# Chunked retention two blocks sooner, and a reordered start, in a retention plus maxout feed-forward kernel

## The chip, the cores and the metric

The kernel runs on one core of a Trainium2 chip. TensorE multiplies matrices into PSUM, VectorE, ScalarE and GpSimd do elementwise work, and SyncE issues most of the transfers between HBM and SBUF. Each engine works through its own queue in order; semaphores order them against each other. The time is device microseconds of one execution. Before the change it is 754.58 us, the median of 12 runs (753.28 to 757.65).

## The reference

```python
def _attn_ref(q, k, v):                    # each (8, 8, 576, 64): batch, heads, sequence, head size
    scores = scale * np.matmul(q, k.transpose(0, 1, 3, 2))
    gamma = 1.0 - 2.0 ** (-5.0 - np.arange(H, dtype=np.float32))
    rel = pos[:, None] - pos[None, :]
    Dmat = np.where(rel >= 0, gamma[:, None, None] ** rel[None, :, :], 0.0)
    return np.matmul(scores * Dmat[None], v)

x = attn_out.transpose(0, 2, 1, 3).reshape(B * S, H * D)          # (4608, 512)
h = np.maximum(np.maximum(x @ w1, x @ w2), x @ w3)                # w1, w2, w3: (512, 768), float64
out = h @ w_out                                                   # w_out: (768, 512), float64
```

Queries, keys and values are float32. The four weight matrices arrive as float64 and are turned into float32 on the chip, by bit operations.

## The kernel before, in words

**Blocks and tiles.** The 4608 rows are cut into 36 blocks of 128 rows (`C`), four blocks (`CPT`) to a tile of 512 rows (`NT`), nine tiles. A sequence has 576 rows, so a block may begin or end in the middle of one. Blocks go through retention, which leaves `xT`; then `ffn(t)` does a tile's three up products, their maximum and the down product.

**Retention of a block in full form** (blocks 0 to 7, lines 258 to 430). `transposes` turns `k` and `q` with TensorE (block 7 with VectorE), and ScalarE copies the result out of PSUM; `decay` multiplies the values by a power of gamma on GpSimd; `scores` makes 128x128 scores per head, which VectorE masks (`st`); `state` makes the product of keys and values that the next blocks need, `keep` adds it to the carried state on VectorE and scales it on GpSimd; `values` multiplies masked scores by values (line 393) and adds the carried state times queries (line 406). `output` scales that into `xT`.

**Retention in chunked form** (from block `BY_CHUNKS` = 8). A block is two chunks of 64. `chunk_scores` makes 64x64 scores (`sk`, line 307) and chunk states (`kv`, line 310), VectorE masks the one (line 314) and adds the other into `stacked` states (lines 322 to 328), with a GpSimd product for every second chunk; `chunk_values` multiplies (lines 424 and 431). `q` and `k` come from HBM in 32-wide pieces (`load_blocks`), so that VectorE can transpose them in 32x32 squares; `k` is loaded a second time as it lies. Blocks from `BY_PE` = 7 on are transposed by VectorE. `carry(8)` brings the full-form state into the stacked form.

**Weights.** `load_weights(n)` issues the next `n` of 24 blocks of 128 float64 rows or columns, 512 KB each; two make a piece pair (`Two(n)`, n from 0 to 11; the last three belong to `w_out`). `convert_all` is a generator whose steps go to VectorE and ScalarE: exponent (line 630) with ScalarE's low word (632), fraction (639) with ScalarE's two steps (638, 641), whole (644), sign (648), product (656), which leaves float32 weights and issues the loads of two later blocks. `convert(n)` takes n steps. Pairs 0 to 2 are converted in halves, the others in one.

**Tile 0.** It is done plainly: nine units of two up products each (`up_plain`, four 512-column products of 3.5 us in sum, line 784, then a copy by ScalarE for the first weight matrix or a maximum by VectorE for the others), then `downs_plain` (line 771). Unit u takes the weights of pair u. Tiles 1 to 8 use sums of weights, inputs and hidden values that cut the number of products (`up`, `downs`, lines 760 and 557).

**Order.** It is written by hand: a preamble does blocks 0 to 3 and the first conversion steps; then for each tile t, `steps(t + 1)` lists twelve groups of loading and retention steps of the next tile's blocks, and between the groups the generator `ffn(t)` is advanced by one unit. What the program lists first stands first in each engine's queue, and on SyncE's queue transfers stand in that same order.

```python
    load_weights(1)        # preamble; before this: load(0) to load(3), of which load(3) also has one
    load(CPT)
    load_weights(4)
```

Of the kernel before, what the change touches and what calls it, by code (L numbers as in the profile page):

```python
# [45 lines left out]
ALU = mybir.AluOpType  # L46
PSUM = bass.MemoryType.PSUM

C = 128
NT = 4 * C  # L50
NH = NT // 2
BY_PE = 7
BY_CHUNKS = 8
AHEAD = 3
FILL = 160
PARTS = 11
# [25 lines left out]
def kernel(  # L82
# [21 lines left out]
    NDC = DM // P  # L104
    NF = DF // P
    CPT = NT // C
    assert B * S % C == 0 and S % D == 0 and BY_CHUNKS % CPT == 0 and S >= C and N % NT == 0 and NT % P == 0 and 2 * D == P and NP == NDC

    const = ctx.enter_context(tc.tile_pool(name="const", bufs=1))
    raw = ctx.enter_context(tc.tile_pool(name="raw", bufs=AHEAD + 1))  # L110
# [14 lines left out]

    gk = const.tile([C, H], FP32, name="gk")
    gs_of = const.tile([P, H], FP32, name="gs_of")
    gs = const.tile([P, NP], FP32, name="gs")  # L130
# [1 line left out]
    const.tile([P, FILL // 4], FP32, name="fill")  # L132
    gq = const.tile([P, NP, C], FP32, name="gq")
    nc.scalar.dma_start(gk[:], key_decay)
    nc.vector.memset(one[:], 1.0)
    nc.scalar.copy(first[:], one[:])

# [31 lines left out]
    def spans(g):  # L169

        row = 0
        while row < C:
# [1 line left out]
            n = min(C - row, S - pos)  # L174
            yield row, b, pos, n
            row += n

    def half(j):
        return slice(D * j, D * (j + 1))

    def place(g, c):

# [39 lines left out]
                        t[r:r + 32, :, e, :],  # L222
                        src[b, :, pos:pos + 32, 32 * a:32 * a + 32].rearrange("h p i -> p h i"))

    def load(g):
        if g >= BY_PE and ("q", g) not in raws:
            load_blocks(g, *range(C // 32))
        for n, src in (("k", k), ("q", q), ("v", v)) if g < BY_PE else (("k", k), ("v", v)):
            if n == "v" and g == CPT - 1:
                load_weights(1)  # L230
            bufs = {"k": 3, "q": 2, "v": 4}[n]
            pool, bufs = (raw0, 1) if n != "v" and g < BY_PE and g % (bufs + 1) == bufs else (raw, bufs)
            if n == "v":
                t = vpool.tile([C, H, D], FP32, tag="v", name="vraw")
            else:
                t = pool.tile([C, H, D], FP32, tag=n, name=n + "raw", bufs=bufs)
            raws[n, g] = t
            for row, b, pos, m in spans(g):
                nc.sync.dma_start(t[row:row + m], src[b, :, pos:pos + m, :].rearrange("h p d -> p h d"))
# [100 lines left out]
    def state_factors():  # L340
        for j in range(2):
            nc.scalar.copy(gs_of[half(0), j::2], gs[half(j)])
# [386 lines left out]
    def convert(n):  # L729
        for _ in range(n):  # L730
            next(converting, None)
# [44 lines left out]
                    nc.sync.dma_start(out[t * NT + m * P:t * NT + (m + 1) * P, :], osb[:])  # L776
            yield

    def up_plain(t, h, fb, i):
        ps = (ps_x, ps_y)[fb % 2].tile([P, NT], FP32, tag="xy"[fb % 2], name="up")  # L780
        first_of_all = t == 0 and (fb, i) == (0, 0)
        for cols in (slice(0, NT - C), slice(NT - C, NT)) if first_of_all else (slice(0, NT),):
            for dc in range(NDC):
                nc.tensor.matmul(ps[:, cols], lhsT=w_sb[i, fb][:, dc * P:(dc + 1) * P], rhs=xT[t][:, dc, cols],  # L784
                                 start=dc == 0 and cols.start == 0, stop=dc == NDC - 1,
                                 skip_group_check=first_of_all)
        if i > 0:
            return lambda: nc.vector.tensor_tensor(h[:, fb, :], h[:, fb, :], ps[:], op=ALU.max)
        return lambda: nc.scalar.copy(h[:, fb, :], ps[:])

    def ffn(t):

        h = hpool.tile([P, NF, NT], FP32, tag="h", name="h")
        if t == 0:
            for fp, i in units:
                for fb in (2 * fp, 2 * fp + 1):
                    maximum = up_plain(t, h, fb, i)
                    if CPT not in qks:
                        maximum()
                        transposes(CPT)  # L800
                        convert(4)
                        continue
                    if (fp, i) == units[-1]:
                        maximum()
                        convert(2)
                        continue
                    convert(4 if (fp, i) in units[:2] else 2)
                    maximum()
                yield
            convert(3)  # L810
            for fb, _ in enumerate(downs_plain(t, h)):
                convert(2 if fb < 2 else 4 * len(pieces))
                if fb == 2:
                    while_converting.close()
                    late["pool"] = ctx.enter_context(tc.tile_pool(name="late", bufs=1))
                    late_room()
                    sums_of_outs()
                elif fb > 2:
                    chore({3: 4, 4: 0, 5: 2}[fb])
                if fb in (1, 3):  # L820
                    yield
            yield
            return
        if t == 1:
            spread.append(True)
            weight_sums(0)
            weight_sums(2)
        plain = 1 if t == 1 else None
        order = (1, 0, 2) if t == 1 else (0, 2, 1)
        total = sum(48 if fp == plain else 2 * len(PRODUCTS) for fp in order)  # L830
        count = parts = 0
        for fp in order:
            if fp != plain:
                while fp not in summed_fp:
                    chore()
            for step, cost in enumerate(up_plain_all(t, h, fp) if fp == plain else up(t, h, fp)):
                if fp == plain:
                    chore(4 if step == 4 else 8)
                elif step % 4 == 1 or step % 4 == 3 and len(urgent) > (2 if t == 1 else 6):
                    chore(len(urgent) > 0)  # L840
                elif step % 4 == 2 and chores and (t > 1 or NF // 2 - 1 not in summed_fp):
                    chores.popleft()()
                if step % 3 == 2:
                    scale()
                count += cost or 1
                if count * (NF // 2 * 3) >= (parts + 1) * total:
                    parts += 1
                    yield
            sums_of_hidden(h, fp)
            if fp == plain:  # L850
                weight_sums(fp)
        chore(len(urgent))
        for n, _ in enumerate(downs(t, h, order)):
            chore(4)
            scale(2)
            if n in (1, 3):
                yield
        yield

    def up_plain_all(t, h, fp):  # L860
        for fb in (2 * fp, 2 * fp + 1):
            for i in range(3):
                up_plain(t, h, fb, i)()
                yield 8


    warm(6)
    for g in range(CPT):
        load(g)
        if g == 1:  # L870
            for j in range(2):
                nc.sync.dma_start(gs[half(j)].unsqueeze(2), state_decay[half(j), :, D * j:D * j + 1])
    load_weights(1)
    load(CPT)
    load_weights(4)
    decay(0)
    transposes(0)
    for c in range(2):
        for b in range(2):
            nc.scalar.dma_start(gq[half(c), b::2, :], out_decay[half(b), NP // 2 * c:NP // 2 * (c + 1), :])  # L880
    warm(2)
    scores(0)
    transposes(1)
# [4 lines left out]
    scores(1)  # L888
    first_output()
    transposes(2)  # L890
    state_factors()
    decay(2)
    state(1)
    keep(1)
    values([1], [1])
    transposes(3)
    decay(3)
    scores(2)
    scores(3)
    state(2)  # L900
    keep(2)
    convert(2)
    values([2], [2])
    convert(2)
    values([3], [3])
    convert(4)
    keep(3)
    decay(CPT)
    convert(2)

    def steps(t):

# [11 lines left out]
        if t == 1:  # L924
            a, b, c, d = range(CPT, 2 * CPT)
            at(0, (load, b))
            at(1, (scores, a), (state, a), (keep, a))
            at(2, (transposes, b), (decay, b), (load, c), (load_weights, 2))
            at(3, (scores, b), (load_blocks, d, 0))
            at(4, (decay, c), (load_blocks, d, 1, 2))  # L930
            at(5, (values, [a, b], [b, c]), (load_blocks, d, 3), (load, d))
            at(6, (keep, c), (transposes, c), (load_blocks, d + 1, 0))
            at(7, (transposes, d), (decay, d), (load_blocks, d + 1, 1, 2))
            at(8, (scores, c), (scores, d), (load_blocks, d + 1, 3), (load, d + 1))
            at(9, (load_blocks, d + 2, 0, 1))
            at(10, (decay, d + 1), (load_blocks, d + 2, 2))
            at(11, (values, [c, d], [d]), (load_blocks, d + 2, 3), (load, d + 2),
               (transposes, d + 1))
            return todo
        for n in range(0, CPT, 2):  # L940
            a, b, m = CPT * t + n, CPT * t + n + 1, 6 * (n // 2)
            first_pair = a == BY_CHUNKS
            s = m + 2 if first_pair else m + 1
            at(m - (t == 2 and n > 0), (transposes, b))
            if first_pair:
                at(m, (decay, b), (load, a + 2), (carry, a))
            at(s, (scores, a), (scores, b), (load, b + 2))
            at(s + 1, (decay, a + 2))
            at(s + 2, (decay, b + 2))
# [60 lines left out]
```

## Time and profile before

| | |
|---|---|
| median of 12 runs | 754.58 us |
| the profiled execution | 753.82 us |
| its span, first to last instruction | 751.8 us |
| TensorE clock granted | 1.00 |
| HBM read, written | 48.76 MB, 9.44 MB |
| first up product starts | 24.90 us |
| last product of tile 0's down ends | 123.68 us |
| VectorE transposes of block 7 | 0.70 and 0.67 us |
| largest wait of TensorE | 1.5 us |

A line of a timeline has the start, the length, the engine, the line of the program, the operation, output and inputs by their names with the shape, the number of instructions merged, and in brackets the idle time before it with what ended it. TensorE takes two instructions for each float32 product of the program. A line of waits has the engine and operation that waited, what it waited for, and then microseconds in total, how often, and the longest. A line of windows has the stretch, its length, the busy time of TensorE, its weight loads, VectorE, ScalarE and GpSimd with instruction counts, the clock, the busy share of the DMA engines and the GB/s moved.

### The profile page before, as it was taken

Reading aid. Unit: us, or ns where it says so; the run is one execution under the profiler, and the core shown is the slowest. Engines: PE = TensorE matmul, PEld = TensorE weight load, DVE = VectorE, ACT = ScalarE, POOL = GpSimd, SP = SyncE. Lnnn points to the kernel's source line nnn. Section 1 sums busy time; section 2 is a strip of 40 time slices with the busy share of each in tenths; the row PEclk is TensorE's granted clock in tenths of the full one; section 3 lists DMA queues with packets and bytes.
Section 4 is the critical chain, followed back from the end, with each engine's and each line's share of the span. In section 5 each row is a group of like instructions: output and inputs, shape, how many; then the busy total and the mean of one; then the engine's idle time right before and its main releaser. Section 6 shows DMA issues by size and latency. Waiting matters only on the chain.

```text
span 751.8 us, 16566 instructions
## 1 busy us (share of the span) xinstructions
PE 744.8 (99%) x6728; PEld 608.1 (81%) x6728; DVE 509.6 (68%) x856; ACT 319.7 (43%) x645; POOL 83.3 (11%) x103
## 2 busy tenths in 40 slices
PE   9899999999999999999999999999999999999998
PEld 7545545588888888888888888888888888888887
DVE  3998987857866765686567746775667656763662
ACT  3574531155245433644254335542454245414441
POOL 3110122002000100011010101010101010100000
PEclk9999999999999999999999999999999999999999
DMA  9996842515142514242343224232515151000001
GB/s 230 224 245 135 224 91 73 97 17 99 44 93 43 94 39 96 50 76 52 72 86 67 61 66 91 48 67 67 96 27 95 44 98 31 1 30 29 0 1 57
DMA packets 230204, 59.30 MB, mean 79 GB/s; under 512 B 210800, under 2 KB 228848, under 8 KB 230128
## 3 DMA queue, kind: packets, MB, share of 16 engines
q1 hardware_dynamic: 229264, 57.91, 35.7%
q8 instruction: 53, 0.87, 0.5%
q10 hardware_dynamic: 864, 0.33, 0.2%
q14 instruction: 23, 0.19, 0.1%
HBM read 48.76 MB, written 9.44 MB: 77 GB/s over the span
## 4 chain that ended last, share of the span: by engine, by line
PE 97%; DVE 1%; DMA 1%; SPq 0%; issue 0%; ACT 0%; ACTq 0%; DVEq 0%
PE a L760 19%; PE b L760 16%; PE dx L557 11%; PE up L784 11%; PE c L760 8%; PE dz L557 6%; PE e L760 5%; PE d L760 5%; PE sk L307 3%; PE down L771 3%; PE dy L557 3%; PE o L424 2%; PE o L431 2%; PE s L285 1%; PE kv L310 1%; PE o L393 1%
## 5 line engine op out<-in xcount | busy, mean ns | idle before, releaser
L748 DVE TENSOR_TENSOR part<-part 128x512 f32<-128x512 f32 x161 | 111.2, 691 | 107.8 <-ACT part L745 105.4
L745 ACT COPY part<-b 128x512 f32<-128x512 f32 x115 | 67.4, 586 | 154.0 <-PE b L760 154.0
L748 DVE TENSOR_TENSOR h<-h,part 128x512 f32<-128x512 f32 x115 | 79.6, 693 | 28.9 <-ACT h L745 24.9
L784 PE MATMUL up<-xT,w 128*128 128x512 f32 (+2 forms) x200 | 84.9, 579 | 1.5 <-DVE w L656 1.5
L745 ACT COPY part<-a 128x512 f32<-128x512 f32 x92 | 53.9, 586 | 49.4 <-PE a L760 49.1
L784 PEld LDWEIGHTS up<-xT,w 128*128 128x128 f32 x200 | 36.7, 190 | 43.7 <-issue 39.9
L760 PE MATMUL a<-s,w 128*128 128x256 f32 x276 | 70.9, 379 | 0.0
L760 PE MATMUL b<-s,n 128*128 128x256 f32 x276 | 70.8, 379 | 0.0
L189 ACT ACTIVATE vraw<-vraw,gk 128x64 f32<-128x64 f32 x208 | 65.5, 346 | 1.6 <-DMA vraw<-in_v_dram 1.6
L760 PEld LDWEIGHTS b<-s,n 128*128 128x128 f32 x276 | 52.4, 190 | 7.1
L760 PEld LDWEIGHTS a<-s,w 128*128 128x128 f32 x276 | 52.4, 190 | 7.1
L527 POOL TENSOR_TENSOR H<-h 128x256 f32<-128x256 f32 x24 | 20.2, 842 | 310.1 <-DVE h L748 310.1
L760 PE MATMUL c<-xT,w 128*128 128x256 f32 x184 | 49.1, 389 | 0.0
L760 PE MATMUL b<-xT,n 128*128 128x256 f32 x184 | 47.2, 379 | 0.0
L760 PE MATMUL d<-s,w 128*128 128x256 f32 x184 | 47.2, 379 | 0.0
L324 POOL TENSOR_TENSOR s<-s,gs_of 64x512 f32<-64x512 f32 x21 | 22.4, 1069 | 211.1 <-DVE s L322 209.2
L557 PE MATMUL dx<-To,H 128*128 128x256 f32 (+1 forms) x204 | 44.9, 370 | 0.0
L760 PE MATMUL e<-xT,w 128*128 128x256 f32 x184 | 43.5, 379 | 0.0
L760 PE MATMUL a<-xT,n 128*128 128x256 f32 x184 | 43.5, 379 | 0.0
L557 PEld LDWEIGHTS dx<-To,H 128*128 128x128 f32 x204 | 36.6, 190 | 4.9
L760 PEld LDWEIGHTS e<-xT,w 128*128 128x128 f32 x184 | 35.0, 190 | 5.2 <-issue 0.2
L760 PEld LDWEIGHTS b<-xT,n 128*128 128x128 f32 x184 | 35.0, 190 | 4.8
(122 smaller groups left out, 1287.6 us busy)
## 6 DMA issues: line engine op xcount, KB each, us to landing
bits<-in_moe_w_dram SPq DMA_DIRECT2D x36, 256.0 KB, 5.6
out_dram<-osb SPq DMA_DIRECT2D x35, 256.0 KB, 2.1
kraw<-in_k_dram SPq DMA_DIRECT2D x32, 256.0 KB, 3.0
vraw<-in_v_dram SPq DMA_DIRECT2D x32, 256.0 KB, 3.5
qraw<-in_q_dram SPq DMA_DIRECT2D x224, 32.0 KB, 2.2
kxraw<-in_k_dram SPq DMA_DIRECT2D x224, 32.0 KB, 2.1
bits<-in_moe_w_out_dram SPq DMA_DIRECT2D x6, 512.0 KB, 6.0
qraw<-in_q_dram SPq DMA_DIRECT2D x6, 256.0 KB, 4.4
```

Source lines behind the costliest of these rows:

```text
L189: scaling.popleft()()
L307: nc.tensor.matmul(s[half(c), h, :], lhsT=kT[half(c), h, :], rhs=qT[half(c), h, :], start=True, stop=True)
L324: nc.gpsimd.tensor_tensor(new, new, factor, op=ALU.mult)
L424: nc.tensor.matmul(o[m][half(c), n, u, :], lhsT=vds[g][half(m), h, :], rhs=sts[g][half(m), h, :], start=n == 0 and u == 0, stop=place(g, m ...
L431: nc.tensor.matmul(o[m][half(c), n, u, :], lhsT=stacks[g][half(m), h, :], rhs=qks[g]["q"][half(m), h, :], start=False, stop=True, skip_gro ...
L527: urgent.append(lambda: (pool(s3, a11, a21, op=ALU.subtract), pool(s4, a12, s2, op=ALU.subtract)))
L557: nc.tensor.matmul(o, lhsT=hS[n](fp)[:, m * P:(m + 1) * P], rhs=late["T"][n][:, fp, cols], start=first and fp == order[0] and (m == 0 or l ...
L745: nc.scalar.copy(of[step], ps[step[0]][:])
L748: nc.vector.tensor_tensor(of[dst], a, b, op=op)
L760: nc.tensor.matmul(ps[chain][:, e, :], lhsT=factor(w, 2 * fp + e), rhs=xS[t][x], start=n == 1 and e == 0, stop=ends, skip_group_check=True)
L771: nc.tensor.matmul(b[:], lhsT=h[:, fb, m * P:(m + 1) * P], rhs=w_sb["out", fb], start=(fb == 0), stop=(fb == NF - 1))
L784: nc.tensor.matmul(ps[:, cols], lhsT=w_sb[i, fb][:, dc * P:(dc + 1) * P], rhs=xT[t][:, dc, cols], start=dc == 0 and cols.start == 0, stop= ...
```

## The change

Blocks 6 and 7 go over to the chunked form (`BY_CHUNKS` 8 to 6), and block 6 is transposed by VectorE (`BY_PE` 7 to 6). `carry` runs for block 6. The schedule of tile 1's blocks follows: block 6's loads become 32-wide pieces, no full state of blocks 6 and 7 is made, and two more conversion steps are taken in group 5.

The start is reordered: the state factors `gs` and half of the output factors `gq` are issued on ScalarE's queue earlier; the first weight block stands before block 2's values on SyncE, the second before block 3's values, two more before block 4; block 2 is scored before block 3 is transposed; conversion steps are spread between. The first two up products are each cut into 384 and 128 columns (`first_ups`), and the last block of the tile gets its state and values between them, so that the 384-column parts need blocks 0 to 2 alone.

```diff
-BY_PE = 7
-BY_CHUNKS = 8
+BY_PE = 6
+BY_CHUNKS = 6
...
     nc.scalar.dma_start(gk[:], key_decay)
+    for j in range(2):
+        nc.scalar.dma_start(gs[half(j)].unsqueeze(2), state_decay[half(j), :, D * j:D * j + 1])
...
+    def first_ups(h):
+
+        g = CPT - 1
+        rest0, copy0 = up_plain(0, h, 0, 0, g * C)
+        convert(2)
+        state(g)
+        convert(2)
+        values([g])
+        keep(g)
+        convert(2)
+        rest1, copy1 = up_plain(0, h, 1, 0, g * C)
+        convert(2)
+        for step in (rest0, copy0, rest1, copy1):
+            step()
+        decay(CPT)
+        transposes(CPT)
+        convert(4)
...
             for fp, i in units:
+                if (fp, i) == units[0]:
+                    first_ups(h)
+                    yield
+                    continue
                 for fb in (2 * fp, 2 * fp + 1):
-                    maximum = up_plain(t, h, fb, i)
-                    if CPT not in qks:
-                        maximum()
-                        transposes(CPT)
-                        convert(4)
-                        continue
-                    if (fp, i) == units[-1]:
+                    maximum, = up_plain(t, h, fb, i)
+                    if (fp, i) == units[-1] and fb % 2:
                         maximum()
                         convert(2)
-                        continue
-                    convert(4 if (fp, i) in units[:2] else 2)
-                    maximum()
+                    else:
+                        convert(4 if (fp, i) == units[1] else 2)
+                        maximum()
...
     warm(6)
-    for g in range(CPT):
-        load(g)
-        if g == 1:
-            for j in range(2):
-                nc.sync.dma_start(gs[half(j)].unsqueeze(2), state_decay[half(j), :, D * j:D * j + 1])
+    load(0)
+    load(1)
+    load(2, "kq")
     load_weights(1)
+    load(2, "v")
+    load(CPT - 1, "kq")
+    load_weights(1)
+    load(CPT - 1, "v")
+    load_weights(2)
     load(CPT)
-    load_weights(4)
+    load_weights(2)
     decay(0)
-    transposes(0)
-    for c in range(2):
+
+    def output_factors(c):
         for b in range(2):
             nc.scalar.dma_start(gq[half(c), b::2, :], out_decay[half(b), NP // 2 * c:NP // 2 * (c + 1), :])
+
+    output_factors(0)
+    transposes(0)
+    output_factors(1)
...
     values([1], [1])
-    transposes(3)
-    decay(3)
     scores(2)
-    scores(3)
+    decay(CPT - 1)
+    convert(2)
     state(2)
     keep(2)
+    convert(1)
+    values([2], [2])
+    transposes(CPT - 1)
+    convert(1)
+    state_factors()
     convert(2)
-    values([2], [2])
-    convert(2)
-    values([3], [3])
-    convert(4)
-    keep(3)
-    decay(CPT)
-    convert(2)
+    scores(CPT - 1)
...
             at(0, (load, b))
-            at(1, (scores, a), (state, a), (keep, a))
-            at(2, (transposes, b), (decay, b), (load, c), (load_weights, 2))
-            at(3, (scores, b), (load_blocks, d, 0))
-            at(4, (decay, c), (load_blocks, d, 1, 2))
-            at(5, (values, [a, b], [b, c]), (load_blocks, d, 3), (load, d))
-            at(6, (keep, c), (transposes, c), (load_blocks, d + 1, 0))
-            at(7, (transposes, d), (decay, d), (load_blocks, d + 1, 1, 2))
-            at(8, (scores, c), (scores, d), (load_blocks, d + 1, 3), (load, d + 1))
+            at(2, (scores, a), (state, a), (keep, a), (transposes, b), (decay, b), (load_weights, 2))
+            at(3, (scores, b), (load_blocks, c, 0, 1))
+            at(4, (load_blocks, c, 2, 3), (load, c))
+            at(5, (values, [a, b], [b]), (convert, 2), (load_blocks, d, 0, 1))
+            at(6, (carry, c), (transposes, c), (decay, c), (load_blocks, d, 2, 3), (load, d))
+            at(7, (transposes, d), (decay, d), (load_blocks, d + 1, 0, 1))
+            at(8, (scores, c), (scores, d), (load_blocks, d + 1, 2, 3), (load, d + 1))
             at(9, (load_blocks, d + 2, 0, 1))
             at(10, (decay, d + 1), (load_blocks, d + 2, 2))
-            at(11, (values, [c, d], [d]), (load_blocks, d + 2, 3), (load, d + 2),
+            at(11, (values, [c, d]), (load_blocks, d + 2, 3), (load, d + 2),
                (transposes, d + 1))
...
             if first_pair:
-                at(m, (decay, b), (load, a + 2), (carry, a))
+                at(m, (decay, b), (load, a + 2))
```

More of the change, by code (lines that the diff above doesn't have):

```diff
@@ L106 @@
     CPT = NT // C
-    assert B * S % C == 0 and S % D == 0 and BY_CHUNKS % CPT == 0 and S >= C and N % NT == 0 and NT % P == 0 and 2 * D == P and NP == NDC
+    assert B * S % C == 0 and S % D == 0 and BY_CHUNKS % 2 == 0 and S >= C and N % NT == 0 and NT % P == 0 and 2 * D == P and NP == NDC
     const = ctx.enter_context(tc.tile_pool(name="const", bufs=1))
@@ L124, with half @@
     ctx.enter_context(tc.manual_schedule())
+    def half(j):
+        return slice(D * j, D * (j + 1))
     gk = const.tile([C, H], FP32, name="gk")
@@ L176, in spans @@
             row += n
-    def half(j):
-        return slice(D * j, D * (j + 1))
     def place(g, c):
@@ L223, in load_blocks, with load @@
                         src[b, :, pos:pos + 32, 32 * a:32 * a + 32].rearrange("h p i -> p h i"))
-    def load(g):
+    def load(g, names="kqv"):
         if g >= BY_PE and ("q", g) not in raws:
@@ L228, in load @@
         for n, src in (("k", k), ("q", q), ("v", v)) if g < BY_PE else (("k", k), ("v", v)):
-            if n == "v" and g == CPT - 1:
-                load_weights(1)
+            if n not in names:
+                continue
             bufs = {"k": 3, "q": 2, "v": 4}[n]
@@ L777, in downs_plain, with up_plain, products, maximum @@
             yield
-    def up_plain(t, h, fb, i):
+    def up_plain(t, h, fb, i, *parts):
         ps = (ps_x, ps_y)[fb % 2].tile([P, NT], FP32, tag="xy"[fb % 2], name="up")
-        first_of_all = t == 0 and (fb, i) == (0, 0)
-        for cols in (slice(0, NT - C), slice(NT - C, NT)) if first_of_all else (slice(0, NT),):
+        def products(a, b):
             for dc in range(NDC):
[L784 to L789, printed above, removed]
+                nc.tensor.matmul(ps[:, a:b], lhsT=w_sb[i, fb][:, dc * P:(dc + 1) * P], rhs=xT[t][:, dc, a:b],
+                                 start=dc == 0 and a == 0, stop=dc == NDC - 1, skip_group_check=len(parts) > 0)
+        def maximum():
+            if i > 0:
+                nc.vector.tensor_tensor(h[:, fb, :], h[:, fb, :], ps[:], op=ALU.max)
+            else:
+                nc.scalar.copy(h[:, fb, :], ps[:])
+        ends = [0, *parts, NT]
+        steps = [partial(products, a, b) for a, b in zip(ends, ends[1:])]
+        steps.pop(0)()
+        return (*steps, maximum)
+    def first_ups(h):
[14 more added lines that the diff above has]
+        convert(4)
     def ffn(t):
@@ L795, in ffn @@
             for fp, i in units:
+                if (fp, i) == units[0]:
+                    first_ups(h)
+                    yield
+                    continue
                 for fb in (2 * fp, 2 * fp + 1):
-                    maximum = up_plain(t, h, fb, i)
-                    if CPT not in qks:
-                        maximum()
-                        transposes(CPT)
-                        convert(4)
-                        continue
-                    if (fp, i) == units[-1]:
+                    maximum, = up_plain(t, h, fb, i)
+                    if (fp, i) == units[-1] and fb % 2:
                         maximum()
                         convert(2)
-                        continue
-                    convert(4 if (fp, i) in units[:2] else 2)
-                    maximum()
+                    else:
+                        convert(4 if (fp, i) == units[1] else 2)
+                        maximum()
                 yield
@@ L862, in up_plain_all @@
             for i in range(3):
-                up_plain(t, h, fb, i)()
+                maximum, = up_plain(t, h, fb, i)
+                maximum()
                 yield 8
     warm(6)
-    for g in range(CPT):
-        load(g)
-        if g == 1:
-            for j in range(2):
-                nc.sync.dma_start(gs[half(j)].unsqueeze(2), state_decay[half(j), :, D * j:D * j + 1])
-    load_weights(1)
+    load(0)
+    load(1)
+    load(2, "kq")
+    load_weights(1)
+    load(2, "v")
[3 more added lines that the diff above has]
+    load_weights(2)
     load(CPT)
-    load_weights(4)
+    load_weights(2)
     decay(0)
-    transposes(0)
-    for c in range(2):
+    def output_factors(c):
         for b in range(2):
             nc.scalar.dma_start(gq[half(c), b::2, :], out_decay[half(b), NP // 2 * c:NP // 2 * (c + 1), :])
+    output_factors(0)
+    transposes(0)
+    output_factors(1)
     warm(2)
@@ L890 @@
     transposes(2)
-    state_factors()
     decay(2)
@@ L941, in steps @@
             a, b, m = CPT * t + n, CPT * t + n + 1, 6 * (n // 2)
-            first_pair = a == BY_CHUNKS
+            first_pair = a == 2 * CPT
             s = m + 2 if first_pair else m + 1
```

## The prediction

> **What bounds the kernel now.** I read the page first, then TensorE's waits, its timeline, and the other engines in the stretches that the change touches.
>
> ```profile
> span 751.8 us, 16566 instructions
> ...
> PE 744.8 (99%) x6728; PEld 608.1 (81%) x6728; DVE 509.6 (68%) x856; ACT 319.7 (43%) x645; POOL 83.3 (11%) x103
> ...
> PE 97%; DVE 1%; DMA 1%; SPq 0%; issue 0%; ACT 0%; ACTq 0%; DVEq 0%
> ```
>
> TensorE is nearly never idle and carries 97% of the chain that ended last. So a gain is TensorE work removed, or TensorE idle time filled. Its waits in the first 120 us say how little there is to fill:
>
> ```profile
> PE up L784 <- DVE w L656: 1.5, 1, 1.5
> PE warm L153 <- POOL ident masks.py:199: 1.4, 1, 1.4
> PE o L393 <- POOL vd L249: 0.6, 1, 0.6
> PE down L771 <- DVE w_out L656: 0.4, 1, 0.4
> ```
>
> Who could become the next bound is seen from busy times by stage (PE, PEld, DVE, ACT, POOL, clock, DMA share):
>
> ```profile
> 20.00:66.00 46.00, 43.90 (x244) 23.62 (x244) 43.80 (x66) 30.93 (x38) 6.08 (x6) 1.00 0.98 224
> 66.00:100.00 34.00, 33.64 (x180) 17.06 (x177) 28.40 (x35) 15.41 (x16) 4.40 (x4) 1.00 0.70 172
> ```
>
> From 20 to 66 us VectorE, which converts the float64 weights, is busy 95% and the DMA engines are full. From TensorE's and VectorE's timelines: unit 3's weights were ready at 50.13 and used at 50.48, unit 4's at 57.46 and used at 57.55. An earlier TensorE gets nothing there unless conversion is earlier too.
>
> **The Trainium skill.** "Perfetto Trace Analysis", Identifying the Most-Contended Engine, warns that matmul busy share overstates. The trace agrees: in the head busy intervals overlap, so I take start-to-start times. "TensorE: Matmul & The Clock Gate", Part 3, says small matmuls on different array tiles run together; chunked retention is made of those, and the trace agrees (32 masked-score and 32 state products of two blocks fit in 2.02 us). "DMA: Bandwidth & Descriptors", Issuing engines are not separate DMA queues: scalar and sync transfers share the 16 engines; moving `gs` saves issue time only (SyncE spent 1.63 us on it at 5.56). "GPSIMD Engine Reference", Specifications: its SBUF interface is shared with VectorE. The trace agrees: the exponent step took 1.12 us beside the 1.04 us `vd` product at 20.18, and 0.42 us at 25.43.
>
> **The change, part by part.** A: blocks 6 and 7 chunked. The rows are TensorE's timeline, first column the start:
>
> ```profile
> 66.37 1.10 PE L352 MATMUL kv<-vd,kraw 128*64 128x64 f32 x32
> 67.41 0.90 PE L406 MATMUL o<-qT,state 64*64 64x64 f32 x32
> ...
> 75.21 0.60 PE L271 MATMUL kt<-ident,kraw 128*128 128x128 f32 x4
> 75.64 0.60 PE L271 MATMUL qt<-ident,qraw 128*128 128x128 f32 x4
> 76.08 13.90 PE L784 MATMUL up<-xT,w 128*128 128x512 f32 x32
> ...
> 113.31 1.97 PE L393 MATMUL o<-st,vd 128*64 128x128 f32 x32
> 115.11 0.63 PE L352 MATMUL kv<-vd,kraw 128*64 128x64 f32 x16
> 115.68 1.10 PE L406 MATMUL o<-qT,state 64*64 64x128 f32 x32
> 116.71 7.13 PE L771 MATMUL down<-w_out,h 128*128 128x512 f32 x16
> ```
>
> Block 6's transposes leave TensorE: 76.08-75.21 = 0.87. Its full state product goes, half of (67.41-66.37): 0.52. Scores of the pair took 1.98 (89.91 to 91.89); chunked scores with states 2.02 (137.51 to 139.53): +0.04. Values: 116.71-113.31 = 3.40 becomes 2.02 (156.95 to 158.97): -1.38. Sum 0.87+0.52-0.04+1.38 = **2.73 us less TensorE work**. That is certain, since the same operations run for blocks 8 and 9. ScalarE loses two 0.59 copies and the two-part carry moves to block 6. VectorE gains a transpose pair (0.70+0.67), two masks and four chunk additions of 0.68 for four 0.62 masks and two 0.41 states: 1.37+4.08-2.48-0.82 = +2.15 us, and GpSimd two 64x512 products of 1.07 for two of about 0.9.
>
> B: the head. Before, the first up product waits at 24.90 for `w` (finished 24.85), whose exponent began at 20.38, since its bits landed at 18.02 and VectorE ran two blocks' masks first. After, on SyncE the first weight (two issues, 1.55 us) stands before block 2's values, and `gs` is gone: it is issued near 7, after eight 256 KB loads, 2.62 MB in all, which at the head's 230 to 280 GB/s have moved by 12; with up to 2.5 us of sharing with later transfers it lands by 14.5. Block 2's values fall from 13.20 to 15-16.5, `vd` a microsecond later. What is behind them: block 1's carried state on GpSimd, block 2's state and values on TensorE. Nothing waits long, for scores 2 now go first and end near 16, masks near 17.3. Then state 2 and values 2 end at 18.5, transposes 3 at 19.4, scores 3 at 21.3. VectorE: exponent and fraction from 17.3, state 0.42, whole 0.69, two `xT` 0.74, sign 0.68, product 0.69: `w` near 21.3. I take **21.6** for the start of up (0,0) in 384 columns; bounds 20.7 and 23.2 (values landing at 17.4, the 8.1 us that was the longest issue-to-landing of a weight, after 9.3). Block 3's state and values (24.90 less its gap: 0.5+0.95+0.6 = 2.05) now come after it. Before, all blocks and no up stood at 24.90; the same work stands at 21.6+2.05 = 23.65: **gain 1.25**, from -0.35 to 2.15. The second split costs like the first, 3.58 (24.90 to 28.48) against 3.53 (29.35 to 32.88): -0.05.
>
> VectorE is advanced too: at `w` (0,0) it has block 3's masks (1.28) still to do, so 24.85-1.28 = 23.57 against 21.3 to 21.7, about 1.8 us ahead. Unit 4's margin of 0.1 becomes 0.1+1.8-1.25 = 0.65: **no stall there**, narrowly. Weights 2 and 3 now stand before block 4 on SyncE; weight 7 stands behind block 5 and lands at about 39.5 for a use at 40.4. Costed at nothing; half a microsecond late would be taken from the same 0.65.
>
> C: the extra conversion steps. Two are taken before unit 5, so from there weights are ready half a unit (3.5 us) sooner relative to TensorE; the 0.36 us wait before `down` (its product now ends in unit 7) goes: **gain 0.36**. The price is a fuller VectorE. From unit 5 to the end of unit 8, about 66.7 to 96.7 by my times, it has: `xT` and state 1.7, exponent-sign-product 3.1, three pairs of 5.0, half a pair 1.9, six maxima 3.6, transposes 2.6, masks and chunk additions 4.1: **32 us in TensorE's 30**. Its last maximum ends near 99.0. The third tile of `down` takes the PSUM buffer of unit 8's first maximum: needed at 98.4, free at 98.4; the fourth needed at 99.3, free at 99.0. I put **0.3 us** of new wait there, bounds 0 and 1.5 (each 1.23 us step can be 1.64 beside GpSimd, as the 1.64 us sign steps at 70.47 and 77.35).
>
> Also moved: output factors before the first transposes hold ScalarE's first copy some 0.4 us (four issues took 3.20 at 6.11), in exchange for the 2.67 us that block 1's copy waited behind them; both lie under block 2's loads. Block 7's transposed loads are 16 issues rather than 32, block 6's another 16, about 0.5 each: SyncE's sum is equal.
>
> Sum: 2.73 + 1.25 - 0.05 + 0.36 - 0.3 = **4.0 us**. The profiled execution took 753.82 (751.8 span and 2.0 around it), so 749.8 in its terms; it stands 0.76 below the median 754.58, which gives **750.6**. After tile 0 I expect no change: from 116 us on VectorE's sums hang on TensorE's own events and move along.
>
> **Rivals.** Head gain lost: block 2's values come late or `w` does, TensorE gives back the 1.25 and only the removed work counts: 2.73-0.35+0.36-0.3, 752.1. Against: VectorE's queue has 1.6 us waits to fill before 17.65. Head better still: up at 20.7 and no PSUM wait, 2.73+2.15+0.36: 749.3. Against: scores 3 need copies on ScalarE behind two 0.72 conversion steps.
>
> Slower: VectorE's queue stops at block 7's transposes, whose transposed loads stand on SyncE behind out-weights that wait for a sign step near 70.4. I reckon SyncE done with them at 81, landed at 83 (a block took 2.2), needed at 84.3. Each microsecond beyond 1.3, plus the PSUM margin of 0.3, is paid once by TensorE; from 5.6 us late the gain is gone, at 8 late the time is 757. For it: VectorE is in order and the fullest engine there. Against: 16 issues of 0.5 us are half of what this path carried from 55.99 to 79.93. That the change does nothing is excluded by A.
>
> **How the numbers follow.** Likeliest 0.58 (749.4 to 752.0), head lost 0.17, better head 0.16, slower by the late loads 0.05, other waits 0.04 that leave it near the old time. 0.2%, about what a measurement tells, is 1.5 us, so faster means under 753.07: the first three, less 0.05 for the tail of head lost: 0.86; same 0.08; slower 0.06. The range takes in both heads' bounds and part of the PSUM wait's: 748.6 to 753.0.
>
> **What would show it.** Up's first start near 21.6 with 384-column products and no 1.5 us wait for `w`; no block-6 transposes on TensorE; values of 6 and 7 in 2.0 us; `down` starting near 96.5 with no wait for `w_out`, perhaps a short one for a maximum; tile 1's first up product, before at 123.68, near 119.7. Wrong if units 1 to 4 show waits for `w` over 0.5 us in sum, if VectorE waits at a transpose for a load, or if `down` waits over a microsecond for PSUM.

## The result, and the profile after

The changed kernel takes 759.88 us (median of 11 runs, 758.2 to 762.1) against 754.68 before (median of 47 runs): a ratio of 1.0069, 95% interval 1.0059 to 1.0079. It is slower; the forecast was 750.6, and the range ended at 753.0. The profiled execution took 760.72 us, with a span of 758.7. It lies 0.8 above its median and that of before 0.8 below its own, so the two spans differ by 6.9 us where the medians differ by 5.2.

The page after (the total and the busy times, the granted clock in 40 slices, the chain by engine):

```profile
span 758.7 us, 16824 instructions
...
PE 746.7 (98%) x6856; PEld 608.0 (80%) x6856; DVE 512.2 (68%) x858; ACT 318.5 (42%) x643; POOL 85.9 (11%) x103
...
PEclk9989999999999999999999999999999999999999
...
PE 91%; DVE 3%; SPq 2%; DMA 2%; issue 1%; ACT 1%; POOL 0%; DVEq 0%; POOLq 0%; ACTq 0%
```

TensorE's share of the chain fell from 97 to 91%. Its waits in the first 140 us (total, times, longest) say where the rest came in:

```profile
PE qt L273 <- ACT kT L274: 3.2, 1, 3.2
PE down L773 <- DVE h L791: 2.4, 1, 2.4
PE warm L158 <- POOL ident masks.py:199: 1.4, 1, 1.4
PE s L287 <- ACT qT L274: 1.0, 2, 0.7
```

The old waits for `w` and `w_out` are gone; for `vd` 0.3 us is left, at another place. Two larger ones stand at block 5's query transposes and at the third product of `down`. The stretch around the first of them, before the change:

```profile
32.88 1.16 PE L285 MATMUL s<-qT,kT 64*128 64x128 f32 x16
33.97 0.68 PE L352 MATMUL kv<-vd,kraw 64*64 64x64 f32 x16
34.59 7.13 PE L784 MATMUL up<-xT,w 128*128 128x512 f32 x16
41.55 0.60 PE L271 MATMUL kt<-ident,kraw 128*128 128x128 f32 x4
41.99 0.60 PE L271 MATMUL qt<-ident,qraw 128*128 128x128 f32 x4
```

and after:

```profile
39.46 1.16 PE L287 MATMUL s<-qT,kT 64*128 64x128 f32 x16
40.55 0.68 PE L354 MATMUL kv<-vd,kraw 64*64 64x64 f32 x16
41.16 0.66 PE L273 MATMUL kt<-ident,kraw 128*128 128x128 f32 x4
44.98 1.11 PE L273 MATMUL qt<-ident,qraw 128*128 128x128 f32 x4 [3.16 <-ACT kT L274]
45.88 9.15 PE L786 MATMUL up<-xT,w 128*128 128x512 f32 x16
54.96 1.16 PE L287 MATMUL s<-qT,kT 64*128 64x128 f32 x16
```

The second, before:

```profile
99.38 14.00 PE L771 MATMUL down<-w_out,h 128*128 128x512 f32 x32 [0.36 <-DVE w_out L656]
```

and after:

```profile
102.98 1.88 PE L773 MATMUL down<-w_out,h 128*128 128x512 f32 x4
107.31 13.98 PE L773 MATMUL down<-w_out,h 128*128 128x512 f32 x28 [2.44 <-DVE h L791]
121.22 1.16 PE L426 MATMUL o<-m,vraw 64*64 64x64 f32 x64
```

Unit 2, the row at 45.88, runs 9.08 us to the next start where it ran 6.96 before. The windows of this kernel (last three columns: granted clock, DMA share, GB/s) show why:

```profile
44.00:46.00 2.00, 1.02 (x5) 1.02 (x6) 2.00 (x5) 0.92 (x2) 0.00 (x0) 0.50 1.10 249
46.00:48.00 2.00, 2.00 (x4) 0.89 (x4) 1.97 (x3) 1.87 (x3) 0.00 (x0) 0.50 1.11 243
48.00:50.00 2.00, 2.00 (x3) 0.67 (x2) 0.71 (x1) 1.97 (x3) 0.00 (x0) 0.50 1.12 247
50.00:52.00 2.00, 2.00 (x6) 0.90 (x5) 0.37 (x1) 1.16 (x2) 0.00 (x0) 0.97 1.11 247
...
108.00:110.00 2.00, 2.00 (x4) 0.76 (x3) 1.97 (x3) 1.48 (x2) 0.00 (x0) 0.54 0.44 68
110.00:112.00 2.00, 2.00 (x4) 0.87 (x3) 1.90 (x3) 0.81 (x1) 0.00 (x0) 0.61 0.74 161
```

TensorE is granted half its clock from 43.3 to 50.1, of which it works 5.1 us, and again from 108.2 to 111.6, 3.4 us. So each wait of 3.16 and 2.44 us is paid nearly twice. From TensorE's start times in the two profiled executions:

| stretch | before | after | change |
|---|---|---|---|
| start to unit 1, without block 4's scores and state | 32.88 | 32.50 | -0.38 |
| scores and state of block 4, transposes of 5 | 2.59 | 6.42 | +3.83 |
| unit 2 | 6.96 | 9.08 | +2.12 |
| scores 5 to values of 4 and 5 | 18.84 | 18.21 | -0.63 |
| units 5 to 8, with what lies between | 31.15 | 29.81 | -1.34 |
| `down` up to the values of 6 and 7 | 13.93 | 18.24 | +4.31 |
| values of 6 and 7 | 3.40 | 2.02 | -1.38 |

The sum is +6.53 at tile 1's first up product (123.68 to 130.21); what follows adds 0.4. The gains are 3.73 us, where 2.73+1.25-0.05+0.36 = 4.29 were forecast. The two waits with their slow clock cost 10.26.

### The profile page after: what moved, and what is told of

Same layout as the page of the kernel before. It is cut to its first block, busy times and chain, and to the rows that moved or that the text cites. A ratio compares the mean times of both kernels' runs of the same rounds, so it can differ in the third digit from the quotient of the medians.

```text
span 758.7 us, 16824 instructions
## 1 busy us (share of the span) xinstructions
PE 746.7 (98%) x6856; PEld 608.0 (80%) x6856; DVE 512.2 (68%) x858; ACT 318.5 (42%) x643; POOL 85.9 (11%) x103
## 4 chain that ended last, share of the span: by engine, by line
PE 91%; DVE 3%; SPq 2%; DMA 2%; issue 1%; ACT 1%; POOL 0%; DVEq 0%; POOLq 0%; ACTq 0%
PE a L762 18%; PE b L762 16%; PE dx L559 11%; PE c L762 8%; PE dz L559 5%; PE up L786 5%; PE d L762 5%; PE e L762 5%; PE sk L309 3%; PE down L773 3%; PE dy L559 3%; PE o L426 2%; PE o L433 2%; SPq L241 1%; PE kv L312 1%
## 5 line engine op out<-in xcount | busy, mean ns | idle before, releaser
L786 PE MATMUL up<-xT,w 128*128 128x512 f32 (+2 forms) x208 | 86.7, 573 | 0.2 <-PE s L287 0.2
L786 PEld LDWEIGHTS up<-xT,w 128*128 128x128 f32 x208 | 38.6, 194 | 43.4 <-issue 39.6
L326 POOL TENSOR_TENSOR s<-s,gs_of 64x512 f32<-64x512 f32 x23 | 24.9, 1084 | 220.5 <-DVE s L324 217.0
```

The costliest lines, as they stand in the source:

```text
L326: nc.gpsimd.tensor_tensor(new, new, factor, op=ALU.mult)
L786: nc.tensor.matmul(ps[:, a:b], lhsT=w_sb[i, fb][:, dc * P:(dc + 1) * P], rhs=xT[t][:, dc, a:b], start=dc == 0 and a == 0, stop=dc == NDC - ...
```

## The experiments

Theory P for the first wait: the pool `ps_r` has four PSUM buffers. Each tile takes one, and a fifth tile has to wait until the first has been read. In group 2 block 4's two score tiles, its state and block 5's key transposes now follow each other directly and fill it; the query transposes are the fifth tile and wait until VectorE's mask has read the first score tile. Before, the scores stood one group earlier, with a 7 us unit between. VectorE and ScalarE of the changed kernel:

```profile
40.97 0.69 DVE L632 TENSOR_SCALAR expo<-bits 128x1024 int32<-128x1024 int32 x1 [0.99 <-DMA bits<-in_moe_w_dram]
41.58 0.69 DVE L641 TENSOR_SCALAR frac<-bits 128x1024 int32<-128x1024 int32 x1
42.37 1.23 DVE L646 SCALAR_TENSOR_TENSOR mant<-frac,mant 128x1024 f32<-128x1024 int32 x1
43.51 0.68 DVE L791 TENSOR_TENSOR h<-h,up 128x512 f32<-128x512 f32 x1
44.11 1.28 DVE L203 TENSOR_TENSOR st<-s,causal 128x512 f32<-128x512 f32 x2
...
40.96 1.27 ACT L634 ACTIVATE mant<-bits,one 128x1024 f32<-128x1024 uint32 x1 [2.93 <-DMA bits<-in_moe_w_dram]
```

The first mask ends near 44.8, and the query transposes start at 44.98. The profile names ScalarE's copy (44.36 to 44.93), which ended last. Theory D: the new order of loads brings pair 3's bits late, which the waits of 0.99 and 2.93 us here speak for.

**head_only.** The new start, retention and groups as before.

```diff
-BY_PE = 6
-BY_CHUNKS = 6
+BY_PE = 7
+BY_CHUNKS = 8
...
-            at(2, (scores, a), (state, a), (keep, a), (transposes, b), (decay, b), (load_weights, 2))
+            at(1, (scores, a), (state, a), (keep, a))
+            at(2, (transposes, b), (decay, b), (load, c), (load_weights, 2))
```

> The changed kernel's start with the retention of before (blocks 6 and 7 in full form, tile 1's groups as before, so block 4 is scored one group ahead of block 5's transposes). Theory P (in the changed kernel TensorE stood at block 5's transposes because block 4's scores, its state and both transposes fill the four PSUM buffers of one pool, and the fifth tile waits for VectorE's mask, which stands behind pair 3's conversion): no wait there, unit 2 takes 7.0 us, about 754.3 us. Theory D (the wait comes from the new order of loads, which brings pair 3's weights late): TensorE waits at block 5's transposes or for unit 2 or 3 all the same, about 759.

753.97 us, ratio 0.9989 (0.9981 to 0.9998); no wait at the transposes, clock 1.00. The start alone is a small gain, and its order of loads alone makes no wait there.

**chunks_only.** The start of before with the changed constants and groups (the other half of the diff).

> The start of before with the changed retention and groups. P: block 4's scores and state stand right ahead of block 5's transposes, so TensorE waits for VectorE's mask there, about 4 us and a lower clock after it, and again before the down product for a maximum: 758 to 762 us. D: pair 3's bits are on time, no wait at the transposes, the 2.7 us of removed work are gained and only the wait at the down product is paid: about 756.

758.25, ratio 1.0049 (1.0029 to 1.0068), with waits of 2.08 at the transposes and 2.55 at `down`. Both waits belong to the retention part. D falls as the main cause.

**scores_early.**

```diff
-            at(2, (scores, a), (state, a), (keep, a), (transposes, b), (decay, b), (load_weights, 2))
+            at(1, (scores, a), (state, a), (keep, a))
+            at(2, (transposes, b), (decay, b), (load_weights, 2))
```

> The changed kernel with block 4's scores, state and keep one group earlier, as they were before. P: the 3.16 us wait at block 5's query transposes goes, and with it unit 2's stretch from 7.0 to 9.1 us: 759.9-3.8-2.1 = 754.0 us. D: pair 3's bits still land near 41 us and TensorE waits about as long, 759 or more.

754.42, ratio 0.9999 (0.9991 to 1.0008). The transposes follow each other in 0.44 us, unit 2 takes 6.97; the wait at `down` stays, 2.43.

**bits_early.**

```diff
-            at(0, (load, b))
+            at(1, (load, b))
```

> The changed kernel with block 5's loads one group later, so that the weights of pair 3 stand ahead of them. D: the wait at block 5's transposes and the slow unit after it go, about 754 us. P: VectorE's mask comes only the 1.0 us sooner that it waited for bits, the wait shrinks from 3.16 to about 2.2 us: 757.5 to 759; block 5's queries landing later may take it back.

758.26, ratio 1.0053 (1.0035 to 1.007). The wait shrinks and is now named after the mask itself:

```profile
43.73 0.66 PE L273 MATMUL qt<-ident,qraw 128*128 128x128 f32 x4 [1.77 <-DVE st L203]
```

Late bits lengthened the wait by 1 to 1.4 us; they did not make it.

**before_adjacent.** The kernel before, with that one group changed.

```diff
-            at(1, (scores, a), (state, a), (keep, a))
-            at(2, (transposes, b), (decay, b), (load, c), (load_weights, 2))
+            at(2, (scores, a), (state, a), (keep, a), (transposes, b), (decay, b), (load, c), (load_weights, 2))
```

> The kernel before with one edit: block 4's scores, state and keep stand in group 2, right ahead of block 5's transposes. P (four PSUM buffers, the fifth tile waits for VectorE's mask): a wait of 2 to 4 us at block 5's query transposes, and a lower clock after it in some executions: 757 to 760. If the wait needs something of the new start or of the chunked blocks, 754.6 as before.

760.07, ratio 1.0054 (1.0037 to 1.0071): one moved group makes the kernel of before slower by most of what the whole change did. The profile is of the slowest of its four runs; 1.6 of the 7.2 us that its span is longer arose in the start, ahead of the moved group (block 4's transposes at 30.05, before at 28.48).

```profile
44.08 0.66 PE L271 MATMUL kt<-ident,kraw 128*128 128x128 f32 x4
47.53 0.66 PE L271 MATMUL qt<-ident,qraw 128*128 128x128 f32 x4 [2.80 <-ACT kT L272]
48.02 8.73 PE L784 MATMUL up<-xT,w 128*128 128x512 f32 x16
```

**other_buffer.** The changed kernel with its order untouched; one tile comes from another pool.

```diff
-            pool, tag = (ps_r, "r") if g >= CPT else (ps_x, "x")
+            pool, tag = (ps_r, "r") if g >= CPT and (n, g) != ("q", CPT + 1) else (ps_x, "x")
```

> The changed kernel, its order of work untouched; only the PSUM tile of block 5's query transposes comes from the pool of the up products (two buffers, one of them free then) in place of the pool of four. P (the fifth tile of the pool of four waits until VectorE's mask has read the first): the 3.16 us wait and the slow unit behind it go, 754 to 755 us, as with block 4's scores one group earlier. If ScalarE's late copy of the keys, which the profile names, were the cause, TensorE would stand as long, 759 or more.

753.12, ratio 0.9987 (0.9974 to 0.9999). In the profiles its lead over scores_early has two main parts: with the scores behind unit 1 TensorE does not wait 0.78 us for ScalarE's copies of block 4, and the wait at `down` is 1.62. This buffer together with the later chunked scores of the run both, below, was not run. The first wait is shown to be that buffer:

```profile
40.90 0.66 PE L273 MATMUL kt<-ident,kraw 128*128 128x128 f32 x4
41.39 0.60 PE L273 MATMUL qt<-ident,qraw 128*128 128x128 f32 x4
41.83 7.03 PE L786 MATMUL up<-xT,w 128*128 128x512 f32 x16
```

**fill.** Is it the standing still that brings the clock down?

```diff
                 nc.tensor.transpose(pt[:, p, :], pair(src, p), ident[:C, :C])
+            if g == CPT + 1 and n == "k":
+                warm(14)
```

> The changed kernel with 14 idle products of the identity (0.22 us each, 3.1 us) on TensorE between block 5's key and query transposes, where it stood still for 3.16 us; their result is used by nothing. If the lower clock behind the wait comes from standing still: unit 2 takes 7.0 us again, 759.9-2.1 = 757.8. If the clock falls for another reason: 759.9 or up to 3 us more where the products add to the wait.

```profile
41.71 3.29 PE L158 MATMUL warm<-ident 128*128 128x128 f32 x28
45.60 0.66 PE L273 MATMUL qt<-ident,qraw 128*128 128x128 f32 x4 [0.60 <-ACT kT L276]
46.09 7.03 PE L788 MATMUL up<-xT,w 128*128 128x512 f32 x16
53.05 1.16 PE L289 MATMUL s<-qT,kT 64*128 64x128 f32 x16
```

In the profile unit 2 takes 6.96 again, at full clock. The mean clock agrees in all four runs: 0.998 three times and 1.00 once, against 0.993 to 0.996 in ten of the changed kernel's twelve. The time, 759.78 with ratio 1.0050 (1.0033 to 1.0068), missed the 757.8 expected and does not settle it: the interval touches that of the change, the transposes started 0.6 later, and another 0.7 was lost to block 7's values.

For the second wait, VectorE of the changed kernel:

```profile
98.57 0.68 DVE L791 TENSOR_TENSOR h<-h,up 128x512 f32<-128x512 f32 x1
99.17 0.69 DVE L316 TENSOR_TENSOR m<-sk,low 128x512 f32<-128x512 f32 x1
99.89 1.41 DVE L324 TENSOR_TENSOR s<-kv,s 64x512 f32<-64x512 f32 x2
101.33 0.69 DVE L316 TENSOR_TENSOR m<-sk,low 128x512 f32<-128x512 f32 x1
102.54 1.41 DVE L324 TENSOR_TENSOR s<-kv,s 64x512 f32<-64x512 f32 x2 [0.52 <-POOL s L326]
103.98 0.69 DVE L641 TENSOR_SCALAR frac<-bits 128x1024 int32<-128x1024 int32 x1
104.78 1.88 DVE L646 SCALAR_TENSOR_TENSOR mant<-frac,mant 128x1024 f32<-128x1024 int32 x1
106.58 1.27 DVE L791 TENSOR_TENSOR h<-h,up 128x512 f32<-128x512 f32 x2
```

Theory M: masks and chunk additions, 99.17 to 103.98 and needed only at 121.22, stand ahead of unit 8's maxima, which free the PSUM buffers of `down`. Rival E: the two extra conversion steps overfill VectorE.

**both.** scores_early, and the chunked scores behind unit 8.

```diff
-            at(8, (scores, c), (scores, d), (load_blocks, d + 1, 2, 3), (load, d + 1))
-            at(9, (load_blocks, d + 2, 0, 1))
+            at(8, (load_blocks, d + 1, 2, 3), (load, d + 1))
+            at(9, (scores, c), (scores, d), (load_blocks, d + 2, 0, 1))
```

> Scores of block 4 one group earlier, and the chunked scores of blocks 6 and 7 one group later (behind unit 8 rather than ahead of it). Theory M (at the down product TensorE waits for the PSUM buffer of unit 8's maximum, because VectorE does the masks and chunk additions of blocks 6 and 7, 4.8 us, ahead of it): the wait of 2.43 us and the doubled products beside it go, 754.4-2.6 = 751.8, with a better start of the units 751.2. Rival E (the two extra conversion steps of group 5 overfill VectorE): the wait stays near 2.4 us and the time near 754.4, since VectorE's sum is the same.

751.17 us, ratio 0.9944 (0.9931 to 0.9956): faster than both kernels. No wait of TensorE after the start exceeds 0.8 us, and `down` runs undisturbed:

```profile
97.84 14.00 PE L773 MATMUL down<-w_out,h 128*128 128x512 f32 x32
111.78 1.16 PE L426 MATMUL o<-m,vraw 64*64 64x64 f32 x64
```

**early_no_extra.** scores_early without `(convert, 2)` in group 5.

> Scores of block 4 one group earlier, and the two extra conversion steps of group 5 taken out. E: the wait at the down product goes, about 751.9. M: masks and additions still stand ahead of unit 8's maxima, and now also ahead of the sign and product of the first down weights, so TensorE waits longer for these, 755 to 757.

755.5, ratio 1.0004 (0.9992 to 1.0016). The wait for the maximum is replaced by one of 2.35 for `w_out`, so leaving the steps out does not help. E falls, also because both lost the wait with the two steps in place.

**early_max_first.** scores_early; in the last unit both maxima come before the conversion steps.

```diff
-                    if (fp, i) == units[-1] and fb % 2:
+                    if (fp, i) == units[-1]:
                         maximum()
-                        convert(2)
+                        convert(4 if fb % 2 else 0)
```

> Scores of block 4 one group earlier; masks and chunk additions stay ahead of unit 8's maxima, but these now come before unit 8's conversion steps (2.5 us, and slowed by GpSimd). M (TensorE waits for the PSUM buffer that unit 8's first maximum frees): in the profile with the wait this maximum would start at 99.3 in place of 101.9, so the wait falls from 2.43 us to 0 to 0.5 and the time from 754.4 to about 752.3; the later down weights may cost some tenths. If the buffer is not what is waited for, no change.

752.29, ratio 0.9971 (0.9959 to 0.9982), as expected; no wait listed at `down`. The buffer freed by the maximum is what `down` waited for.

**chunks_mended.** chunks_only with the group edits of both.

> The start of before, the chunked blocks 6 and 7 with both mends (block 4's scores one group earlier, the chunked scores one group later). It shows what part A of the prediction is worth without the waits: 2.73 us of removed work and the 0.36 us wait for down weights, 755.0-3.1 = 751.9; if the new start is needed to keep the units supplied with weights, waits for weights at units 2 to 4 and 753 or more.

751.43, ratio 0.9958 (0.9943 to 0.9973). The retention part is worth 0.42% without its waits, and needs nothing of the new start. What the start adds in both (0.9944 against 0.9958) is within the intervals.

**both_no_extra.** both without `(convert, 2)`.

> Both mends on the changed kernel, without the two extra conversion steps. Prediction's part C gave these steps 0.36 us (no wait for the first down weights): 751.2+0.4 = 751.6. If they only fill VectorE, 751.2 or less.

A miss: 756.18, ratio 1.002 (1.0012 to 1.0028).

```profile
PE down L773 <- DVE w_out L658: 3.0, 1, 3.0
...
108.18 7.13 PE L773 MATMUL down<-w_out,h 128*128 128x512 f32 x16 [3.01 <-DVE w_out L658]
```

With the chunked scores in group 9 the masks stand ahead of pair 10's product, and `down` needs that at its third block. The two extra steps, which I had valued at 0.36 us, bring the product ahead of the masks: there they are worth about 5 us.

## Why the prediction was wrong

**Part A held.** The stretches from scores 5 to unit 8 and the values of 6 and 7 gave 0.63+1.34+1.38 = 3.35 us, against 2.73 and the 0.36 of part C. Without the waits, by two edits that the prediction did not have, the kernel reaches 751.17, near the 750.6 forecast.

**Part B failed where its sum has no term, between unit 1 and unit 2.** It went through the weights for the units and VectorE's order up to block 3's masks; I did not count the PSUM tiles of group 2. The move of block 4's scores next to block 5's transposes is in the diff, four buffers are in the pool's line, and five tiles follow each other. Cost: 3.83 us, and 2.12 through the clock. The "no stall there, narrowly" was said of unit 4's weights, and held: no unit waited for `w`. Pair 3's bits, "costed at nothing" for a landing at 39.5, came only near 40.9 and added 1 us to the wait for the buffer.

**The head gave less in the profile.** 1.25 was forecast, 0.38 came. The first up product started at 22.32, not 21.6. Block 2's values ended at 19.16 instead of 18.5, so scores 3 ended at 22.1; and the product that leaves `w` took 1.52 us instead of 0.69, beside two GpSimd products, and ended at 22.17. The two 0.72 us conversion steps that I had named against the better head were not in the way: ScalarE made its copies as soon as block 3's transposes ended. In time head_only gained 0.11%, 0.2 to 1.4 us by its interval, which does not exclude the forecast.

**Part C had the right place and too small a size.** At the third tile of `down` I put 0.3 us, at most 1.5; it was 2.44 of waiting and 4.31 in all, past the microsecond that I had named as a sign of being wrong. VectorE's 32 us were 34.1 and 0.5 of waiting for GpSimd (73.28 to 107.85): steps of 1.23 took 1.88 to 1.95 beside GpSimd three times, and 1.64 once. With a margin of nought, 2.6 us more became a 2.4 us wait.

**A term was missing: the clock.** The sum had none for TensorE running at half clock after it has stood: 2.12 us behind the first wait, and most of the 1.9 us by which the cost at `down`, 4.31, exceeds the wait there. The Trainium skill has it ("TensorE: Matmul & The Clock Gate", HAM oscillation): TensorE should have no idle gap beyond some 3.4 us, or it goes back to half clock. Here gaps of 2.08 to 3.16 us were enough in some executions (last section).

**The slower rival was another one.** Block 7's transposes, at 91.20, did not wait for their loads. The chance of a slower kernel, 0.06, rested almost wholly on that, though VectorE's queue order was what failed, in two places.

## What to carry to other kernels

When steps are moved in a hand-written order, count the tiles of each PSUM pool between a tile and its re-use: the instruction that frees the buffer may stand deep in another engine's queue. On an engine that serves several purposes, work that is not due soon should not stand ahead of work that frees a buffer. A wait of the bounding engine may cost nearly twice its length: here 5.95 us for 3.16, and 4.31 for 2.44.

## What the runs showed of the hardware

In each profile the granted clock changed only at instants that lie whole multiples of 3.41 us apart. In the changed kernel it fell at 43.30, rose at 50.13 (two such steps), fell at 108.16 (nineteen steps after the first fall) and rose at 111.57 (one step). Every other fall before the end of a kernel lasted one step. TensorE stood from 41.82 to 44.98 and from 104.86 to 107.31: the first fall came within the wait, the second 0.85 us behind it. So a wait's length alone does not decide. The table lays the waits over these steps:

| wait of TensorE | us | most of it within one step | next step at half clock |
|---|---|---|---|
| fill, at `down` | 2.62 | 2.62 | yes |
| chunks_only, at `down` | 2.55 | 2.55 | yes |
| changed kernel, at `down` | 2.44 | 2.44 | yes |
| early_no_extra, at `down` | 2.35 | 2.32 | yes |
| bits_early, at `down` | 2.48 | 2.30 | yes |
| before_adjacent, at the transposes | 2.80 | 2.19 | yes |
| chunks_only, at the transposes | 2.08 | 2.08 | yes |
| both_no_extra, at `down` | 3.01 | 1.98 | no |
| scores_early, at `down` | 2.43 | 1.79 | no |
| bits_early, at the transposes | 1.77 | 1.77 | no |
| changed kernel, at the transposes | 3.16 | 1.67 | yes, and the step before too |
| other_buffer, at `down` | 1.62 | 1.62 | no |

No shorter wait was followed by a fall. Eleven of the twelve fit a limit between 1.98 and 2.08 us of standing within one step; no run was made to test it. The first wait of the changed kernel does not fit, and why stays open.

Where the steps lie differs by execution, so the same wait is paid in some and not in others. One step at half clock loses 1.7 of some 755 us, which makes a mean clock of 0.998: scores_early's profile has none, yet two of its 12 runs show 0.998 and took 755.6 and 756.0; both_no_extra's profile has none, yet 16 of its 20 runs show 0.998 or less. The changed kernel's runs spread over 4 us, those of both over 0.7. That standing still is the cause is supported by this table and by the clock of fill, not by fill's time.
